# Sorted block attention and a feed-forward layer on one core: q of batch 1 loaded in rows and turned by TensorE, and w_in loaded in row blocks

## The chip, the cores and the metric

The kernel runs on one core of a Trainium2 chip. The metric is device time in microseconds; lower is better. The core has TensorE (PE; its weight loads are shown apart as PEld), VectorE (DVE), ScalarE (ACT), GpSimd (POOL) and SyncE (SP). POOL and SP also issue the DMA transfers here: POOL the loads, which turn f32 into bf16, SP the stores and the DMA transposes.

## The reference

Four batches of eight heads, 768 tokens, head size 64. A small matrix per head (8x8) is normalised five times over rows and columns and then mixes the eight blocks of 96 keys and of 96 values. Each block of 96 queries attends to its own mixed block. All heads of a token side by side are the input of a feed-forward layer with a leaky activation.

```python
P = sort_net                                   # (4, 8, 8, 8)
for _ in range(5):
    P = np.exp(P - np.max(P, axis=-1, keepdims=True))
    P = P / (np.sum(P, axis=-1, keepdims=True) + 1e-09)
    P = P / (np.sum(P, axis=-2, keepdims=True) + 1e-09)
k_sorted = np.einsum('bhij,bhjcd->bhicd', P, k_b)     # k_b, v_b: (4, 8, 8, 96, 64)
v_sorted = np.einsum('bhij,bhjcd->bhicd', P, v_b)
scores = np.matmul(q_b, k_sb.transpose(0, 1, 2, 4, 3)) / 8
...
x = attn_out.transpose(0, 2, 1, 3).reshape(3072, 512)
h = x @ w_in                                          # 512 x 2048
g = np.maximum(h, 0.0) + alpha * np.minimum(h, 0.0)
out = g @ w_out                                       # 2048 x 512
```

## The kernel before

**Order.** Nothing is issued in the order of the Python text. `G.add` records operations with an engine (or a choice of ACT and DVE, `EITHER`), an assumed duration, what they read and write, and a priority. A list scheduler (`schedule`) lays them out by priority and readiness, `search` tries 1,500 random shifts of the priorities and keeps the best layout by its own durations, and `emit` writes each engine's instructions in that order with semaphore waits. Each engine, and each of the two DMA-issuing engines, then works through its own list in order: an instruction that waits holds back everything behind it on its engine. `fill` puts matmuls whose result nobody uses into gaps of PE's list, ahead of the first FFN2 step.

**Loads.** POOL issues q, k and v of batch 0 first, in rows: the destination has 128 partitions with 3072 consecutive elements each (`QS`, `KS`, `VST`). Then come w_in in four blocks of 512 columns (L803; block `p` serves the FFN steps `ft` 4p to 4p+3), w_out in two, and k of batch 1. q of batches 1 to 3 goes another way (`load_q`): eight loads, one for each head, into `QN`, with tokens on partitions and 64 consecutive elements a piece, the other half of each 128 columns being zeros (L447).

**Turning q.** The scores need q with the head dimension on partitions (`QTz`). For batch 0, `prep_q` does it on PE: six steps of 16 matmuls of 64x64 against the identity (`pairs`, L540), each followed by a copy on ACT or DVE (L373). In this form one head lies on partitions 0 to 63 and another on 64 to 127, and a score matmul uses one half of the rows (L621). For batches 1 to 3, `turn_q` issues six DMA transposes on SP (L410). There the other 64 rows are zeros, and a score matmul uses all 128 rows (L618).

**k and v.** `prep_k` (six steps a batch, L540) and `prep_v` (eight steps, L583) mix the blocks by matmuls with `BDK`, a block matrix made of P. v is first rearranged by `conv_v` into `VD` (L373; from batch 1 on, all on POOL). From batch 1 on all these steps use one PSUM bank, `BANK_P`, the second bank of `psYP`: a step writes the bank, a copy on ACT or DVE empties it, and the next step follows.

**Attention.** 32 groups `g`, eight a batch, each a block of 96 queries in all heads. For batch 0 the scores are made twice (L621, then L642 and L633), exp is one ACT instruction (L665), and PE turns the result (L699). For batches 1 to 3 (`far`) exp is eight ACT instructions (L654), SP issues a DMA transpose of the weights (`ET`, L659), the output product follows (L674), and SP issues another DMA transpose into `xT` (L692).

**FFN.** Tokens go in chunks of 2, 2, and then 4 groups. `ffn1` (L721: four matmuls of 192 or 384 columns; then ACT L731 and DVE L734) makes one of 16 pieces `ft` of the hidden layer; `ffn2` (L760: four parts of four matmuls of 512 columns) makes 128 tokens of output, which are copied and stored (L774). These steps are put between the attention steps by their priorities.

Of the kernel before, what the change touches and what calls it, by code (L numbers as in the profile page):

```python
# [8 lines left out]
AP = bass.AP  # L9
# [9 lines left out]
DFF = 2048  # L19
KT_TILES = DM // 128  # L20
# [15 lines left out]
def t_pe(*mms):  # L36
    return sum(max(n, m, 64) / 2.4 + 4 for n, m in mms)
# [252 lines left out]
def bass_sinkhorn_attn__then__act_prelu_kernel(  # L290
# [11 lines left out]
    G = _Graph()  # L302
# [13 lines left out]
    EITHER = ("act", "dve")  # L316
# [55 lines left out]
    def copy(e, o, i):  # L372
        return e.activation(o, i, ACTF.Copy) if e is nc.scalar else e.tensor_copy(o, i)  # L373

    def t_either(n, mode=1):
        return {"act": t_act(n), "dve": t_dve(n, mode)}
# [17 lines left out]
        return [(("turned", "turnx")[n % 2], g + n // 2)]  # L394

    def load_q(b, prio):
        if b == 0:
            G.add(POOL, lambda e: e.dma_start(QS[0][:, :], AP(q.tensor, 0, [[3072, 128], [1, 3072]])),
                  load_us, w=[("QS", 0)], prio=prio, dma=(d_q[0], 0))
            return  # L400
        for h in range(H):
            G.add(POOL, lambda e, h=h: e.dma_start(  # L402
                AP(QN, h * 128 + (h // 4) * 64, [[6144, 128], [1024, 6], [1, 64]]),
                AP(q.tensor, b * HB + h * S * D, [[D, 128], [128 * D, 6], [1, D]])),
                660, r=[("QN0", h)] + paced(13, h // 2) * (b == 3), w=[("QN", h)], prio=prio,
                dma=(d_qn[h], 0))

    def turn_q(b, t, prio):
        n = b % 2
        G.add(SYNC, lambda e: e.dma_start_transpose(  # L410
            AP(QTz[n], t * 128, [[6144, 128], [768, 8], [1, 128]]),
            AP(QN, t * 1024, [[6144, 128], [1, 1024]])),
            4500, r=[("QN", h) for h in range(H)] + [("turned", 8 * b - 8 + t)] * (b > 1),
            w=[("QTzt", n, t)] + ([("Q0", u) for u in range(6)] if n == 0 and t == 0 else []),
            prio=prio, dma=(d_qt[t], 0))

    def load_kv(t, src, name, sem, g, b, prio):
# [125 lines left out]
            return inst  # L543
        return f

    def prep_q(u, prio, bank):
        t, off, row, keys = bank
        G.add(PE, pairs(QS[0], 0, u, identb, 0, 128, bank), 372, r=[("QS", 0), "identb"], w=keys, prio=prio)
        o = AP(QTz[0], 8 * u, [[6144, 128], [96, 32], [48, 2], [1, 8]])
        i = AP(t, off, [[row, 128], [2, 32], [1, 2], [64, 8]])  # L550
        G.add(EITHER, lambda e: copy(e, o, i), t_either(512), r=keys, w=[("Q0", u)], prio=prio)

    def prep_k(b, u, prio, bank=BANK_P):
        n = b % 2
# [14 lines left out]
    def conv_v(b, u, prio):  # L569
        o = AP(VD, 8 * u * 64, [[4096, 128], [64, 8], [1, 48]])  # L570
        i = AP(VST[b % 2], 8 * u, [[3072, 128], [1, 8], [64, 48]])
        G.add(POOL if b or u % 3 == 2 else EITHER, lambda e: copy(e, o, i), {"act": 858, "dve": 540, "pool": 720},
              r=[("VST", b % 2)] + [("VST", b % 2, x) for x in range(4)], w=[("VD", u)], prio=prio)

    def prep_v(b, u, prio, bank=BANK_P):
# [20 lines left out]
    def attention(g, prio):  # L596
# [2 lines left out]
        n, m = b % 2, g % 2  # L599
        far, me = b > 0, g % NE  # L600
        nk = 112
        pos = (lambda h4, hp: 2 * h4 + hp) if far else (lambda h4, hp: 4 * hp + h4)
        ld, bk = 4 * NB * BK0, BK0
        kt_keys = [("KT", n, u) for u in range(6)] + ([] if far else ["KTpad"])
        qt_keys = [("QTzt", n, t) for t in range(i * 96 // 128, (i * 96 + 95) // 128 + 1)] if far else \
            [("QTzt", n, t) for t in range(6)] + [("Q0", u) for u in range(6)]
        vs_keys = [("VS1", n)] + [("VS", n, u) for u in range(8)]
        psZ, psZb, banks_o = (psYP, psYPb, ["psY"] + PSP) if g == 1 else (psO, psOb, ["psO0", "psO1"])
        psX, banks_s = (psH, [("psH", x, y) for x in range(2) for y in range(2)]) if g == 1 else (psS, ["psS0", "psS1"])
# [1 line left out]
        def s1(e):  # L611
            inst = None
            for h4 in range(4):
                for hp in range(2):
                    p = pos(h4, hp)
                    o = AP(psX, (p // 4) * 512 + (p % 4) * 96, [[1024, 96], [1, 96]])
                    if far:
                        inst = e.matmul(o, AP(QTz[n], hp * 3072 + h4 * 768 + i * 96, [[6144, 128], [1, 96]]),  # L618
                                        AP(KT[n], (h4 * 8 + i) * bk, [[ld, 128], [64, 2], [1, 48]]))
                    else:  # L620
                        inst = e.matmul(o, AP(QTz[n], hp * 64 * 6144 + h4 * 768 + i * 96, [[6144, 64], [1, 96]]),  # L621
                                        AP(KT[n], hp * 64 * ld + (h4 * 8 + i) * bk, [[ld, 64], [64, 2], [1, 48]]))
            return inst
# [87 lines left out]
    def ffn1(ga, gb, ft, prio):  # L711
        tok, n = ga * BLK, (gb - ga) * BLK
        tb = step[0] % 3
        banks = BANK_H + ([BANK_P] if ga < 2 else [])
        pt, poff, _, keys = banks[step[0] % len(banks)]
        step[0] += 1

        def f(e):
            inst = None
            for kt in range(KT_TILES):  # L720
                inst = e.matmul(AP(pt, poff, [[1024, 128], [1, n]]),  # L721
                                AP(w_in_bf, kt * DFF + ft * 128, [[KT_TILES * DFF, 128], [1, 128]]),
                                AP(xT, kt * XR + tok % XR, [[KT_TILES * XR, 128], [1, n]]),
                                start=(kt == 0), stop=(kt == KT_TILES - 1))
            return inst
        op = G.add(PE, f, t_pe(*[(n, 128)] * 4), r=[("xT", g % 16) for g in range(ga, gb)] + [("w_in", ft // 4)],
              w=keys, prio=prio)
        if not ffn_ops:
            ffn_ops.append(op)

        G.add(ACT, lambda e: e.activation(AP(t1[tb], 0, [[384, 128], [1, n]]),  # L731
                                          AP(pt, poff, [[1024, 128], [1, n]]), ACTF.Relu, scale=-1.0),
              t_act(n), r=keys, w=[("t1", tb)], prio=prio)
        G.add(DVE, lambda e: e.scalar_tensor_tensor(  # L734
            out=AP(hT, ft * RING + tok % RING, [[FT_TILES * RING, 128], [1, n]]),
            in0=AP(t1[tb], 0, [[384, 128], [1, n]]), scalar=AP(omaT, ft, [[16, 128], [1, 1]]),
            in1=AP(pt, poff, [[1024, 128], [1, n]]), op0=AluOpType.mult, op1=AluOpType.add),
            t_dve(n) + 52, r=keys + [("t1", tb), "omaT"],
            w=[("hT", ft, x % (RING // 64)) for x in range(tok // 64, (tok + n) // 64)], prio=prio)
# [52 lines left out]
    sinkhorn()  # L792
    spread([0], -48)
    for u in range(6):
        prep_q(u, -50, (BANK_H + BANK_O + BANK_S)[u])
    for u in range(6):
        prep_k(0, u, -47, BANKS0[(u + 1) % 5])
    for u in range(8):
# [2 lines left out]
        prep_v(0, u, -45, (BANK_O + [BANK_P])[u % 3])  # L801
    for p in range(4):
        G.add(POOL, lambda e, p=p: e.dma_start(  # L803
            AP(w_in_bf, p * 512, [[KT_TILES * DFF, 128], [DFF, KT_TILES], [1, 512]]),
            AP(moe_w_in.tensor, p * 512, [[DFF, 128], [128 * DFF, KT_TILES], [1, 512]])),
            2550, w=[("w_in", p)], prio=-40 + p, dma=(dma_sem("wi%d" % p), 0))
    for p in range(2):
        G.add(POOL, lambda e, p=p: e.dma_start(
# [26 lines left out]
    for g in range(NG + 12):  # L835
        while fp < len(ffn_plan) and ffn_plan[fp][0] < g:
            pr, kind, a = ffn_plan[fp]
            if kind == 0:
                ffn1(*a, pr)
            else:  # L840
                ffn2(*a)
            fp += 1
        if g >= NG:
            continue
        b, i = g // NB, g % NB
        if i == 0 and b + 1 < B:
            if b == 0:
                load_k(1, -21)
            if b < 2:
                load_q(b + 1, 8 * b - 20)  # L850
            if b == 0:
                load_v(1, -19)
        attention(g, g)
        if g == 1:
            spread([1, 2, 3], 1)
        if b + 1 < B:
            for t in range(6 if b == 0 and i == 1 else 0):
                turn_q(1, t, 2 + t / 2)
            if b > 0 and i < 6:
                turn_q(b + 1, i, 8 * b + 2 + i / 2)  # L860
            vu = [(conv_v, b + 1, u) for u in range(3)]
            for u in range(8):
                vu += [(prep_v, b + 1, u)] + [(conv_v, b + 1, u + 3)] * (u < 5)
            units = [(prep_k, b + 1, u) for u in range(6)]
            units = units + vu if b == 0 else vu + units
            for x in range(len(units)):
                if i == (4 + x * 4 // len(units) if b == 0 else 1 + x * 7 // len(units)):
                    f, *a = units[x]
                    f(*a, 8 * b + 2 + x * 5 / len(units) if b else x / 4 if f is prep_k else 4.5 + x / 8)
        if i == 7 and b == 0:  # L870
            load_v(2, -12)
            load_k(2, -11.9)
        if g == 15:
            load_v(3, -4)
            load_k(3, -3.9)
            load_q(3, -2)
# [49 lines left out]
```

## Time and profile before

| | us |
|---|---|
| median of three runs | 256.91 |
| lowest and highest | 255.8, 257.92 |
| the profiled execution, device time | 259.23 |
| its span, from the first to the last instruction | 257.5 |

The profile is of one execution. Times in it count from the start of its span. Its mean granted clock of TensorE was 0.973. Of the span, PE was busy 93%, DVE 65%, ACT 60% and POOL 24%. The costliest groups of PE are the two FFN products (L721, 97.0 us; L760, 80.0 us on `psYP`). The DMA engines moved 32.17 MB in 77,070 packets, 67,808 of them under 512 bytes.

Some landings, from issue to the last byte: `QS` 7.1 us after issue at 1.3; the four w_in blocks 14.3, 16.3, 18.1 and 20.4 us after issues at 4.3, 5.1, 5.8 and 6.5; k of batch 1 31.8 us after 9.4; the eight `QN` loads of batch 1 27.8 us after the first issue (14.3) to some 24 us after the last (23.1); v of batch 1 26.7 us after 23.9. SP issued the six QTz transposes of batch 1 from 46.87 to 63.76 us.

How to read it: a line of the timeline has the start, the duration, the engine, the source line and the operation, with the tiles written and read and the count of merged instructions. A bracket gives idle time of the engine just before and what ended it. Matmuls overlap, so the distance between two starts says more about the cost of a step than its duration.

### The profile page before, as it was taken

To read this page: it belongs to the slowest core of one execution; us is meant where nothing else is said; L and a number is where in the kernel's file an instruction comes from. 1 tells how busy PE (TensorE), PEld (TensorE's weight loads), DVE (VectorE), ACT (ScalarE), POOL (GpSimd) and SP (SyncE) were. 2 spreads that over 40 slices of the span, in tenths; PEclk is the share of its full clock that TensorE was granted. 3 is DMA by queue.
4 is the path that set the end of the run, shared out by engine and by line. 5 is a ranking of instruction groups with operands and counts; after the bars stand their busy time and mean duration, and the time that the engine had idled before them with its cause. 6 is when DMAs were issued, how large, how long until landed. Compare 5 with 4: busy or idle time off the path is not lost.

```text
span 257.5 us, 6566 instructions
## 1 busy us (share of the span) xinstructions
PE 238.7 (93%) x2721; PEld 147.2 (57%) x2752; DVE 166.2 (65%) x330; ACT 154.1 (60%) x419; POOL 61.4 (24%) x89
## 2 busy tenths in 40 slices
PE   7687799979999997989899999999999999999995
PEld 4355577767656564645565565555555565555544
DVE  5773577666676896756887667466477795655510
ACT  4473444555775976758856654857667775555511
POOL 8999000194493020867100000000000000000000
PEclk9997779988999999999999999999999999999999
DMA  5999999999299989999985961212537234201112
GB/s 100 214 203 203 190 217 165 215 173 196 66 89 197 142 128 158 174 179 178 138 141 129 162 136 59 44 45 75 118 93 97 47 95 113 71 5 40 76 44 83
DMA packets 77070, 32.17 MB, mean 125 GB/s; under 512 B 67808, under 2 KB 73200, under 8 KB 77040
## 3 DMA queue, kind: packets, MB, share of 16 engines
q0 software_dynamic: 25168, 13.63, 40.8%
q1 hardware_dynamic: 51872, 18.11, 38.5%
q8 instruction: 21, 0.34, 0.6%
q14 instruction: 9, 0.07, 0.1%
HBM read 27.28 MB, written 6.29 MB: 130 GB/s over the span
## 4 chain that ended last, share of the span: by engine, by line
PE 76%; DMA 8%; POOL 6%; DVE 3%; issue 3%; ACT 3%; POOLq 0%
PE psH L721 28%; PE psYP L760 25%; DMA ET<-Esb 8%; PE psYP L583 4%; PE psS L760 3%; PE psO L674 3%; PE psS L618 3%; PE psS L633 2%; PE psYP L540 2%; ACT Esb L654 1%; POOL QN L447 1%; PE psYP L883 1%; POOL w_in_bf L803 1%; PE psS L642 1%; PE psO L583 1%
## 5 line engine op out<-in xcount | busy, mean ns | idle before, releaser
L734 DVE SCALAR_TENSOR_TENSOR hT<-t,omaT,psH 128x384 bf16<-128x384 f32 (+1 forms) x139 | 77.6, 572 | 41.2 <-ACT t L731 39.7
L721 PE MATMUL psH<-xT,w_in_bf 128*128 128x384 bf16 (+1 forms) x556 | 97.0, 312 | 0.9 <-DVE hT L734 0.7
L731 ACT ACTIVATE t<-psH 128x384 f32<-128x384 f32 (+1 forms) x139 | 62.3, 465 | 42.5 <-PE psH L721 39.8
L760 PE MATMUL psYP<-w_out_bf,hT 128*128 128x512 bf16 x306 | 80.0, 382 | 2.9 <-issue 1.3
L721 PEld LDWEIGHTS psH<-xT,w_in_bf 128*128 128x128 bf16 x556 | 50.9, 98 | 33.9 <-DVE hT L734 5.9
L654 ACT ACTIVATE Esb<-psS,nf 96x96 bf16<-96x96 f32 x192 | 46.3, 344 | 1.5 <-DVE nf L627 1.3
L760 PEld LDWEIGHTS psYP<-w_out_bf,hT 128*128 128x128 bf16 x336 | 30.6, 98 | 27.9 <-issue 0.6
L373 POOL COPY VD<-VST 128x384 bf16<-128x384 bf16 x26 | 22.6, 869 | 33.8 <-DMA VST<-in_v_dram 25.7
L627 DVE TENSOR_REDUCE nf<-psS 96x8 f32<-96x768 f32 x24 | 22.7, 948 | 2.1 <-PE psS L618 1.9
L684 DVE TENSOR_TENSOR xq<-psO,rec 96x512 bf16<-96x512 f32 x31 | 21.3, 687 | 1.1
L402 POOL DMA_DIRECT2D QN<-in_q_dram x24 | 19.8, 845 | 2.3 <-DMA xT<-xq 1.8
L373 ACT ACTIVATE outstg<-psYP 128x512 f32<-128x512 f32 x15 | 9.0, 597 | 12.7 <-PE psYP L760 12.7
L583 PE MATMUL psYP<-BDK,VD 128*64 128x64 bf16 x416 | 12.1, 202 | 3.5 <-issue 2.0
L681 DVE RECIPROCAL rec<-psO 96x8 f32<-96x8 f32 x31 | 6.2, 201 | 13.2 <-PE psO L674 13.1
L373 ACT ACTIVATE VS<-psYP 112x512 bf16<-112x512 f32 x14 | 9.7, 690 | 7.6 <-PE psYP L583 7.2
L583 PEld LDWEIGHTS psYP<-BDK,VD 128*64 128x64 bf16 x416 | 9.1, 114 | 8.6 <-issue 4.2
L618 PEld LDWEIGHTS psS<-KT,QTz 128*96 128x96 bf16 x192 | 11.6, 124 | 3.2 <-ACT Esb L654 0.4
L373 ACT ACTIVATE KT<-psYP 128x512 bf16<-128x512 f32 x13 | 7.8, 597 | 9.5 <-PE psYP L540 9.5
L618 PE MATMUL psS<-KT,QTz 128*96 128x96 bf16 x192 | 12.8, 209 | 0.0
L674 PEld LDWEIGHTS psO<-VS,ET 112*128 112x128 bf16 x192 | 8.6, 98 | 6.4 <-DMA ET<-Esb 3.0
L883 PE MATMUL psYP<-identb 128*128 128x512 bf16 x37 | 11.6, 438 | 0.3 <-ACT identb L373 0.3
L674 PE MATMUL psO<-VS,ET 112*128 112x65 bf16 x192 | 9.9, 194 | 1.6 <-DMA ET<-Esb 1.6
(116 smaller groups left out, 183.3 us busy)
## 6 DMA issues: line engine op xcount, KB each, us to landing
out_dram<-outstg SPq DMA_DIRECT2D x23, 256.0 KB, 2.3
KS<-in_k_dram POOLq DMA_DIRECT2D x3, 768.0 KB, 30.0
VST<-in_v_dram POOLq DMA_DIRECT2D x3, 768.0 KB, 26.7
QN<-in_q_dram POOLq DMA_DIRECT2D x24, 96.0 KB, 6.5
w_in_bf<-in_moe_w_in_dram POOLq DMA_DIRECT2D x4, 512.0 KB, 17.2
w_out_bf<-in_moe_w_out_dram POOLq DMA_DIRECT2D x2, 1024.0 KB, 27.1
QS<-in_q_dram POOLq DMA_DIRECT2D x1, 768.0 KB, 7.1
VST<-in_v_dram POOLq DMA_DIRECT2D x4, 192.0 KB, 5.4
```

Of the source, the lines that this page charges most:

```text
L373: return e.activation(o, i, ACTF.Copy) if e is nc.scalar else e.tensor_copy(o, i)
L402: G.add(POOL, lambda e, h=h: e.dma_start(AP(QN, h * 128 + (h // 4) * 64, [[6144, 128], [1024, 6], [1, 64]]), AP(q.tensor, b * HB + h * S * ...
L583: inst = e.matmul(AP(t, th * 64 * row + off + dd * 64, [[row, 64], [1, 64]]), AP(VD, (8 * u + dd) * 64, [[4096, 128], [1, 64]]), AP(BDK, b ...
L618: inst = e.matmul(o, AP(QTz[n], hp * 3072 + h4 * 768 + i * 96, [[6144, 128], [1, 96]]), AP(KT[n], (h4 * 8 + i) * bk, [[ld, 128], [64, 2], ...
L627: G.add(DVE, lambda e: e.tensor_reduce(AP(nx, 0, [[8, 96], [4, 2], [1, 4]]), AP(psX, 0, [[1024, 96], [512, 2], [96, 4], [1, 96]]), AxisLis ...
L654: inst = e.activation(AP(Esb[me], p * 128, [[1024, 96], [64, 2], [1, 48]]), AP(psX, (p // 4) * 512 + (p % 4) * 96, [[1024, 96], [48, 2], [ ...
L674: inst = e.matmul(AP(psZ, hp * 512 + h4 * 68, [[1024, 128], [1, 65]]), AP(ET[me] if far else Es0[m], pos(h4, hp) * 96, [[800, nk], [1, 128]]),
L684: G.add(DVE, lambda e: e.tensor_tensor(out=AP(xq[me], 0, [[512, 96], [256, 2], [64, 4], [1, 64]]), in0=AP(psZ, 0, [[1024, 96], [512, 2], [ ...
L721: inst = e.matmul(AP(pt, poff, [[1024, 128], [1, n]]), AP(w_in_bf, kt * DFF + ft * 128, [[KT_TILES * DFF, 128], [1, 128]]), AP(xT, kt * XR ...
L731: G.add(ACT, lambda e: e.activation(AP(t1[tb], 0, [[384, 128], [1, n]]), AP(pt, poff, [[1024, 128], [1, n]]), ACTF.Relu, scale=-1.0), t_ac ...
L734: G.add(DVE, lambda e: e.scalar_tensor_tensor(out=AP(hT, ft * RING + tok % RING, [[FT_TILES * RING, 128], [1, n]]), in0=AP(t1[tb], 0, [[38 ...
L760: inst = e.matmul(AP(bank[0], bank[1], [[1024, 128], [1, n]]), AP(hT, ft * RING + tok % RING, [[FT_TILES * RING, 128], [1, 128]]), AP(w_ou ...
```

## The change

q of batch 1 is now loaded as q of batch 0 is, by one load into `QS`, and turned by `prep_q` on PE into `QTz[1]`, with `BANK_P` as its bank. Its scores use the form with half of the rows; exp, the transposes of `ET` and `xT` and the output product stay as they were. Six DMA transposes and eight loads go. `turn_q` stays for batches 2 and 3, whose first step now waits for the readers of the earlier contents of that `QTz`. w_in is loaded in four blocks of 128 rows with all 2048 columns, and as a product needs all rows, each FFN1 step now depends on all four. The q steps of batch 1 are put between its k steps and its v steps, v with priorities from 4 on in place of 4.5, and the duration that the scheduler assumes for a VD copy on POOL goes from 720 to 870.

```diff
     def load_q(b, prio):
-        if b == 0:
-            G.add(POOL, lambda e: e.dma_start(QS[0][:, :], AP(q.tensor, 0, [[3072, 128], [1, 3072]])),
-                  load_us, w=[("QS", 0)], prio=prio, dma=(d_q[0], 0))
+        if b < 2:
+            G.add(POOL, lambda e: e.dma_start(QS[0][:, :], AP(q.tensor, b * HB, [[3072, 128], [1, 3072]])),
+                  load_us, w=[("QS", 0)], prio=prio, dma=(d_q[b], 0))
             return
...
-            w=[("QTzt", n, t)] + ([("Q0", u) for u in range(6)] if n == 0 and t == 0 else []),
+            w=[("QTzt", n, t)] + [("Q", n, u) for u in range(6)] * (t == 0),
...
-    def prep_q(u, prio, bank):
+    def prep_q(b, u, prio, bank=BANK_P):
         t, off, row, keys = bank
         G.add(PE, pairs(QS[0], 0, u, identb, 0, 128, bank), 372, r=[("QS", 0), "identb"], w=keys, prio=prio)
-        o = AP(QTz[0], 8 * u, [[6144, 128], [96, 32], [48, 2], [1, 8]])
+        o = AP(QTz[b], 8 * u, [[6144, 128], [96, 32], [48, 2], [1, 8]])
...
-        G.add(POOL if b or u % 3 == 2 else EITHER, lambda e: copy(e, o, i), {"act": 858, "dve": 540, "pool": 720},
+        G.add(POOL if b or u % 3 == 2 else EITHER, lambda e: copy(e, o, i), {"act": 858, "dve": 540, "pool": 870},
...
-        pos = (lambda h4, hp: 2 * h4 + hp) if far else (lambda h4, hp: 4 * hp + h4)
+        pos = (lambda h4, hp: 2 * h4 + hp) if b > 1 else (lambda h4, hp: 4 * hp + h4)
...
-                    if far:
+                    if b > 1:
                         inst = e.matmul(o, AP(QTz[n], hp * 3072 + h4 * 768 + i * 96, [[6144, 128], [1, 96]]),
                                         AP(KT[n], (h4 * 8 + i) * bk, [[ld, 128], [64, 2], [1, 48]]))
...
-        op = G.add(PE, f, t_pe(*[(n, 128)] * 4), r=[...] + [("w_in", ft // 4)],
+        op = G.add(PE, f, t_pe(*[(n, 128)] * 4), r=[...] + [("w_in", kt) for kt in range(KT_TILES)],
...
-            AP(w_in_bf, p * 512, [[KT_TILES * DFF, 128], [DFF, KT_TILES], [1, 512]]),
-            AP(moe_w_in.tensor, p * 512, [[DFF, 128], [128 * DFF, KT_TILES], [1, 512]])),
+            AP(w_in_bf, p * DFF, [[KT_TILES * DFF, 128], [1, DFF]]),
+            AP(moe_w_in.tensor, p * 128 * DFF, [[DFF, 128], [1, DFF]])),
...
-            for t in range(6 if b == 0 and i == 1 else 0):
-                turn_q(1, t, 2 + t / 2)
...
-            units = units + vu if b == 0 else vu + units
+            units = units + [(prep_q, 1, u) for u in range(6)] + vu if b == 0 else vu + units
...
-                    f(*a, 8 * b + 2 + x * 5 / len(units) if b else x / 4 if f is prep_k else 4.5 + x / 8)
+                    f(*a, 8 * b + 2 + x * 5 / len(units) if b else x / 4 if f is prep_k else 4 + x / 8)
```

The layout is searched anew, so the order of every engine's list changes around these steps too. In POOL's new list, v and q of batch 1 and then seven of the eight QN loads of batch 2 follow k of batch 1, ahead of v and k of batch 2 (before, the QN loads of batch 2 were issued at 71.4 to 78 us).

## The prediction

> **What bounds the kernel now.** The page first: busy shares, slices, and the head of the chain of waits.
>
> ```profile
> PE 238.7 (93%) x2721; PEld 147.2 (57%) x2752; DVE 166.2 (65%) x330; ACT 154.1 (60%) x419; POOL 61.4 (24%) x89
> ...
> PE   7687799979999997989899999999999999999995
> ...
> PEclk9997779988999999999999999999999999999999
> DMA  5999999999299989999985961212537234201112
> ...
> PE 76%; DMA 8%; POOL 6%; DVE 3%; issue 3%; ACT 3%; POOLq 0%
> ```
>
> PE is busy 93% of the span and holds 76% of the chain, while the DMA engines are full or nearly so (9 or 8) from 6 to 64 us and again from 71 to some 135 us. Transfers bind only through what PE waits for, and PE shows few such waits. Next the windows of PE after the first FFN step (32.21 us); columns: length, busy us of PE, PEld, DVE, ACT, POOL, granted clock, DMA share, GB/s.
>
> ```profile
> 52.00:57.00 5.00, 3.94 (x90) 3.10 (x92) 2.91 (x8) 2.44 (x5) 4.63 (x7) 0.96 1.09 192
> 57.00:60.00 3.00, 2.67 (x27) 1.79 (x28) 2.10 (x4) 1.25 (x4) 1.60 (x2) 0.50 1.67 176
> 60.00:72.00 12.00, 11.61 (x211) 8.74 (x211) 7.90 (x18) 9.03 (x26) 5.67 (x7) 1.00 0.47 101
> 72.00:90.00 18.00, 17.32 (x191) 10.32 (x191) 13.28 (x23) 12.94 (x40) 7.38 (x10) 1.00 1.44 153
> 90.00:104.00 14.00, 12.32 (x210) 7.79 (x213) 10.79 (x18) 10.03 (x32) 2.47 (x5) 1.00 1.10 148
> 104.00:130.00 26.00, 23.57 (x254) 13.81 (x253) 18.34 (x33) 18.25 (x57) 14.62 (x19) 1.00 1.47 162
> ```
>
> Idle PE time is 1.06 + 0.33 us in 52 to 60 and 1.68 + 2.43 us in 90 to 130; the other windows after 32 us have 0.3 to 1.1 each, up to the tail. So PE work that is added after 32 us lengthens the kernel by itself, and a gain must come out of those idle stretches. The prices, from PE's timeline: a step costs the distance from its start to the next start (the second number, its duration, also holds the drain).
>
> ```profile
> 46.97 0.44 PE L540 MATMUL psYP<-BDK,KS 64*64 64x64 bf16 x16
> 47.34 0.41 PE L674 MATMUL psO<-VS,Es 112*128 112x65 bf16 x8
> ...
> 48.71 0.38 PE L621 MATMUL psS<-KT,QTz 64*96 64x96 bf16 x8
> 49.02 0.34 PE L699 MATMUL psO<-identb,xq 96*128 96x96 bf16 x4
> ...
> 79.46 1.46 PE L721 MATMUL psH<-xT,w_in_bf 128*128 128x384 bf16 x8
> 80.76 0.52 PE L618 MATMUL psS<-KT,QTz 128*96 128x96 bf16 x8
> 81.21 0.44 PE L583 MATMUL psYP<-BDK,VD 128*64 128x64 bf16 x16
> 81.58 1.48 PE L721 MATMUL psH<-xT,w_in_bf 128*128 128x384 bf16 x8
> 82.99 0.44 PE L583 MATMUL psYP<-BDK,VD 128*64 128x64 bf16 x16
> ...
> 114.39 0.52 PE L618 MATMUL psS<-KT,QTz 128*96 128x96 bf16 x8
> 114.75 1.03 PE L760 MATMUL psYP<-w_out_bf,hT 128*128 128x512 bf16 x4
> ```
>
> Sixteen 64x64 matmuls (L540, the form of the q turns) cost 0.37 us. Scores in row halves (L621) cost 0.31, over the full array (L618) 0.36 here and up to 0.40. The same eight FFN matmuls take 1.30 us ahead of L618 and 1.41 ahead of L583: going over from a full-array step to one in a part of the array costs 0.10 us more. Ahead of L540, L621 and L642 the distances grow by 0.09 to 0.10 as well; the way back is free. The Trainium skill ("TensorEngine Tiling (Array Packing)", Key Properties) says that a change of tiling mode drains TensorE. The trace agrees, at 0.10 us; the page gives no price for it. Its table Theoretical Speedup has up to 2x for small contractions: eight scores in some 0.19 us, by which the sum below would be 1.0 us lower; L621's 0.31 does not agree.
>
> **The change, part by part.**
>
> *q turns on PE.* Six prep_q steps of batch 1: 6 x 0.37 = 2.22 us, in a stretch where PE has next to no idle time. Their six copies go to ACT, 0.57 us each (row of the QTz copies), 3.4 us in all; ACT is busy 1.25 + 9.03 of the 15 us from 57 to 72, 4.7 free, so I take nothing. If that cover were gone they would cost up to 3.4.
>
> *Scores of batch 1.* Eight groups from 0.36-0.40 to 0.31: 8 x 0.07 = -0.56 us.
>
> *Switches.* PE's order in the changed program goes from a full-array step to a partial one 55 times after the first FFN step, 46 times before: 9 x 0.10 = +0.90. With the scores that is +0.34: the row halves pay for themselves at most.
>
> *DMA transposes.* Six QTz transposes leave SP, where they held the queue from 46.87 to 63.76 us. The next in that queue is an output tile, which nobody waits for. The first score of batch 1 (68.08 us) shows no wait for QTz. I take 0; at most the two waits on ET below.
>
> *q loads.* Eight QN loads (landing one after another from 42.1 us, the last at 46.9, 5.7 us behind k of batch 1 at 41.2) become one QS load with rows like KS and VST, which land 3.8 us apart (v of batch 1 at 50.6, then 54.4 and 58.2). In POOL's new order v of batch 1 goes ahead of it: k lands at 41.2 as before, v at 45.0, q at 48.8. The first prep_q stands after the K steps, near 54, so q comes in time by some 5 us. The QN loads of batch 2 move from 71.4-78 us to POOL's early list; q's six turns no longer hold QN. v and k of batch 2 then land near 58 and 61, v as before (58.2) for VD copies that now come later.
>
> *Waits on ET.* PE idled 0.75 us at 113.3 and 0.49 at 126.3 for ET transposes, beside loads and QTz transposes. With the QN packets out of 71-83 and the turns of batch 2 no longer waiting for them the attention groups run earlier; loads of batch 3 stay. Between 0 and -1.24 I take half, -0.62.
>
> *A gap filled.* The first q turn stands between L699 and L642 of group 6, a place that was 0.45 us long for 0.18 us of work: -0.27.
>
> *w_in in row blocks.* Every first FFN step now needs all four blocks. They landed at 18.6, 21.4, 23.9 and 26.9, 2.75 us apart; first use 32.21. A block of 512 KB would take 2.5 us by the KS rows (3.8 for 768 KB) and 3.8 by the QN loads (5.7 for 768 KB); counted from 15.85, one old block ahead of the first landing, the last lands between 25.9 and 31.1, in time by either: 0.
>
> *The end.* The last group's output product (L674, 220.24) is followed in the old order by 7.6 us of PE work that doesn't need its xT, in the new one by 0.25 + 1.30 + 3 x 0.86 = 4.15. xT came 4.5 us after that product (transpose issued at 222.44, landed 2.3 later): +0.35.
>
> Sum: 2.22 - 0.56 + 0.90 + 0.35 - 0.62 - 0.27 = +2.02 us. The profiled execution took 259.23 (span 257.5), so 261.25 on its own terms; it lies 2.32 above the median, near the size of one 2.03 us stall of PE for nothing shown (19.2 us, followed by a clock of 0.62) that I assume for neither side. On the median: 256.91 + 2.02 = 258.9.
>
> **The rivals.**
>
> *Faster: the gaps close.* Half-speed clock followed the idle stretch: 57 to 60 ran at 0.50, which cost some 1.3 us. The Trainium skill ("TensorE: Matmul & The Clock Gate", Part 1) says that the gate follows recent activity over windows of 3.4 us; the rows agree. If the q turns keep PE busy there and lighter queues end the waits in 90 to 130, all of 1.39 + 1.3 + 4.11 = 6.8 us goes: 256.91 + 2.22 - 0.56 + 0.90 + 0.35 - 6.8 = 253.0. For it: POOL, SP and the early queue are relieved. Against: most of that idle time ends on ACT or DVE emptying a bank (KT 0.69, outstg 0.42, VS 0.30 each, hT 0.41 and 0.31), and the change adds such copies. Chance 0.15.
>
> *Slower: one PSUM bank.* K, q and V of batch 1 all go through BANK_P, a matmul step and then a copy: 20 steps now instead of 14. Before, 14 starts spread from 46.97 to 72.56, 1.97 us each; where they stood closest, 1.14 to 1.39. In the new order the last V step stands on PE near 81 us, so the chain decides from (81 - 47) / 19 = 1.79 us a step on. At 1.97 it ends at 84.4: 3.4 us more, 262.3. Against: FFN steps between them set much of the 1.97. Chance 0.20.
>
> *w_in late.* It decides when a block takes over (32.21 - 15.85) / 4 = 4.1 us; each 0.1 us beyond costs 0.4, and at 4.5 the time is 260.5. The slowest row above is 3.8. Chance 0.03.
>
> **How the numbers follow.** 1% is 2.57 us, about what a measurement of this kernel tells from no change: 254.3 to 259.5. The forecast has 0.62, with its own range 256.8 to 261 (waits on ET in full or none, ACT's copies partly bare). A third or so of it lies above 259.5; with the bank and w_in this makes slower 0.38, the gaps make faster 0.15, and 0.47 is within. 254.0 to 262.5 leaves out the best of the first rival and the worst of the second.
>
> **What would show it.** In the page after: PE busy up by 2 to 3 us, L540 with 96 matmuls more that read QS, L618 at 128 and L621 at 120, QTz transposes 12. No wait of L540 for QS, none of L721 for w_in. FFN steps ahead of the scores of batch 1 at 0.10 us more. ET waits near 113 and 126 gone or halved, and L721 waiting some tenths for xT behind the last L674. I am wrong if PE's idle time between 52 and 130 (5.5 us in those four windows) falls by more than 3 us, or if prep_v steps of batch 1 wait on VS or QTz copies for more than 2 us together.

## The result, and the profile after

| | before | after |
|---|---|---|
| median, us | 256.91 | 259.34 |
| lowest and highest of the runs behind it | 255.8, 257.92 | 258.86, 261.15 |
| the profiled execution, device time | 259.23 | 259.97 |
| its span, mean granted clock | 257.5, 0.973 | 258.3, 0.974 |

The ratio is 1.0102, 95% interval 1.0058 to 1.0146: 2.6 us more, between 1.5 and 3.8. Every ratio and interval in this document leaves out the executions that lie over 1.5% above the fastest of their kernel (one of the five of before, ten of the twelve of before_seed8 further down), while the medians in the table of experiments are of all executions. Set side by side, the two profiled executions differ by only 0.7 us, because that of before lay 2.3 above its median and that of after 0.6.

The page of after, busy shares, slices and the head of the chain of waits:

```profile
PE 241.0 (93%) x2816; PEld 147.5 (57%) x2850; DVE 165.8 (64%) x332; ACT 156.3 (61%) x423; POOL 54.7 (21%) x82
...
PE   7688799979999998999999999999999999999995
...
PEclk9996779989999999999999999999999999999999
DMA  5999999994029788999988781231343233310112
...
PE 77%; DMA 9%; ACT 6%; DVE 4%; issue 2%; SPq 0%; POOL 0%
```

PE is busy 2.3 us longer with 95 matmuls more. The DMA row shows the place of the packets that are gone: the tenth to twelfth slice (58 to 77 us) fall from 9, 2 and 9 to 4, 0 and 2. PE's share of the chain did not get smaller by it (76% before). The same windows as before (length, busy us of PE, PEld, DVE, ACT, POOL, granted clock, DMA share, which adds up the times of packets and can pass 1, and GB/s):

```profile
52.00:57.00 5.00, 4.02 (x88) 3.10 (x84) 2.58 (x6) 3.04 (x6) 0.05 (x1) 0.89 1.06 216
57.00:60.00 3.00, 2.67 (x37) 1.68 (x40) 1.97 (x4) 1.41 (x4) 0.00 (x0) 0.61 1.05 144
60.00:72.00 12.00, 11.63 (x221) 8.84 (x220) 6.83 (x17) 9.43 (x27) 2.56 (x3) 1.00 0.08 26
72.00:90.00 18.00, 16.96 (x239) 9.79 (x234) 12.88 (x22) 12.69 (x35) 5.27 (x7) 1.00 0.68 108
90.00:104.00 14.00, 12.76 (x186) 7.29 (x189) 10.63 (x18) 9.86 (x33) 1.65 (x4) 1.00 0.85 121
104.00:130.00 26.00, 24.55 (x275) 14.42 (x278) 19.13 (x33) 19.46 (x61) 14.82 (x19) 1.00 1.45 171
```

Idle PE time in 52 to 60 and 90 to 130 is 0.98 + 0.33 + 1.24 + 1.45 = 4.0 us, 1.5 less than before. The turns and the new switches, from PE's timeline of after (start, duration, then the step):

```profile
52.90 0.34 PE L699 MATMUL psO<-identb,xq 96*128 96x96 bf16 x4
53.66 0.44 PE L540 MATMUL psYP<-identb,QS 64*64 64x64 bf16 x16 [0.41 <-ACT KT L373]
54.03 0.41 PE L642 MATMUL psS<-QTz,KT 64*112 64x96 bf16 x8
...
59.84 0.44 PE L540 MATMUL psYP<-identb,QS 64*64 64x64 bf16 x16
60.21 0.41 PE L642 MATMUL psS<-QTz,KT 64*112 64x96 bf16 x8
...
108.74 1.46 PE L721 MATMUL psH<-xT,w_in_bf 128*128 128x384 bf16 x8
110.13 0.38 PE L621 MATMUL psS<-KT,QTz 64*96 64x96 bf16 x8
110.44 0.44 PE L540 MATMUL psYP<-BDK,KS 64*64 64x64 bf16 x16
```

A turn costs 0.37 us (59.84 to 60.21), a score group of batch 1 now 0.31 (110.13 to 110.44), and an FFN1 step of eight matmuls ahead of it 1.39 in place of 1.30. The first turn waited 0.41 us for the bank. Of PE's waits in after, summed over the kernel (us in total, times, the longest):

```profile
PE psH L721 <- DVE hT L734: 1.1, 3, 0.5
...
PE psYP L540 <- DVE KT L373: 0.5, 1, 0.5
PE psYP L540 <- ACT KT L373: 0.4, 1, 0.4
PE psO L674 <- DMA ET<-Esb: 0.4, 1, 0.4
...
PE psYP L583 <- DVE VS L373: 0.2, 1, 0.2
```

The three ET waits of before (1.6 us) are one of 0.4. No turn of batch 1 waits for QS and no FFN1 step for w_in. Of the bank's waits 0.41 and 0.16 us fall into the preparation of batch 1; the 0.5 belongs to batch 2.

Counting from the first FFN1 step (32.21 us before, 31.75 after) to the end of the last PE step (254.85, 255.61), after takes 223.86 us and before 222.64. Taking all start-to-start distances of that stretch, less the idle time printed in brackets, PE's steps come to 216.06 before and 218.38 after, its idle time to 6.58 and 5.48. So the work grew by 2.3 us, and gaps took up 1.1 of it in these two executions. Of the idle time 1.3 and 1.4 us stand ahead of L760 with no releaser, and they are in doubt: these two traces have 369 and 366 of the 400 matmuls of L760, and the four traces that have all 400 show no such idle time.

### The profile page after: what moved, and what is told of

Same layout as the page of the kernel before. It is cut to its first block, busy times and chain, and to the rows that moved or that the text cites. A ratio compares the mean times of both kernels' runs of the same rounds, so it can differ in the third digit from the quotient of the medians.

```text
span 258.3 us, 6752 instructions
## 1 busy us (share of the span) xinstructions
PE 241.0 (93%) x2816; PEld 147.5 (57%) x2850; DVE 165.8 (64%) x332; ACT 156.3 (61%) x423; POOL 54.7 (21%) x82
## 4 chain that ended last, share of the span: by engine, by line
PE 77%; DMA 9%; ACT 6%; DVE 4%; issue 2%; SPq 0%; POOL 0%
PE psH L721 29%; PE psYP L760 25%; DMA VST<-in_v_dram 5%; PE psS L760 3%; PE psYP L540 3%; PE psO L674 3%; ACT Esb L654 3%; PE psYP L583 3%; PE psS L633 2%; PE psS L618 2%; DMA ET<-Esb 2%; ACT t L731 2%; PE psYP L881 1%; DVE hT L734 1%; PE psS L621 1%
## 5 line engine op out<-in xcount | busy, mean ns | idle before, releaser
L760 PE MATMUL psYP<-w_out_bf,hT 128*128 128x512 bf16 x303 | 78.7, 382 | 3.4 <-issue 1.4
L721 PEld LDWEIGHTS psH<-xT,w_in_bf 128*128 128x128 bf16 x556 | 50.2, 98 | 34.9 <-DVE hT L734 5.9
L760 PEld LDWEIGHTS psYP<-w_out_bf,hT 128*128 128x128 bf16 x336 | 30.4, 98 | 29.3 <-issue 0.5
L373 POOL COPY VD<-VST 128x384 bf16<-128x384 bf16 x26 | 22.9, 879 | 42.4 <-PE psYP L583 22.5
L373 ACT ACTIVATE outstg<-psYP 128x512 f32<-128x512 f32 x16 | 9.6, 597 | 14.3 <-PE psYP L760 14.3
L402 POOL DMA_DIRECT2D QN<-in_q_dram x16 | 13.3, 853 | 7.0 <-DMA xT<-xq 5.7
L373 DVE CAST VS<-psYP 112x512 bf16<-112x512 f32 x11 | 7.6, 689 | 7.6 <-PE psYP L583 7.6
L373 ACT ACTIVATE VS<-psYP 112x512 bf16<-112x512 f32 x15 | 10.3, 688 | 3.3 <-PE psYP L583 2.9
L583 PE MATMUL psYP<-BDK,VD 128*64 128x64 bf16 x416 | 11.7, 200 | 0.2 <-DVE VS L373 0.2
L583 PEld LDWEIGHTS psYP<-BDK,VD 128*64 128x64 bf16 x416 | 8.8, 113 | 5.3 <-issue 2.9
L373 ACT ACTIVATE KT<-psYP 128x512 bf16<-128x512 f32 x12 | 7.2, 596 | 6.2 <-PE psYP L540 6.1
L618 PEld LDWEIGHTS psS<-KT,QTz 128*96 128x96 bf16 x128 | 7.9, 124 | 2.8 <-ACT Esb L654 0.8
```

The source lines that it names most:

```text
L402: G.add(POOL, lambda e, h=h: e.dma_start(AP(QN, h * 128 + (h // 4) * 64, [[6144, 128], [1024, 6], [1, 64]]), AP(q.tensor, b * HB + h * S * ...
L583: inst = e.matmul(AP(t, th * 64 * row + off + dd * 64, [[row, 64], [1, 64]]), AP(VD, (8 * u + dd) * 64, [[4096, 128], [1, 64]]), AP(BDK, b ...
L721: inst = e.matmul(AP(pt, poff, [[1024, 128], [1, n]]), AP(w_in_bf, kt * DFF + ft * 128, [[KT_TILES * DFF, 128], [1, 128]]), AP(xT, kt * XR ...
L760: inst = e.matmul(AP(bank[0], bank[1], [[1024, 128], [1, n]]), AP(hT, ft * RING + tok % RING, [[FT_TILES * RING, 128], [1, 128]]), AP(w_ou ...
```

## The experiments

Each run stands beside runs of the kernel before on the same chip; their medians were 257.78, 259.03 and 257.84 in the three sittings. Ratios are to those.

| kernel | median, us | ratio and 95% interval |
|---|---|---|
| after_again (w_in in columns) | 259.18 | 1.0088, 1.0045 to 1.0130 |
| q_twice | 262.72 | 1.0187, 1.0123 to 1.0252 |
| q_one | 259.12 | 1.0044, 1.0003 to 1.0085 |
| full_rows | 259.43 | 1.0079, 1.0037 to 1.0121 |
| w_rows_alone | 257.93 | 1.0019, 0.9976 to 1.0062 |
| copy_doubled | 260.27 | 1.0133, 1.0080 to 1.0187 |
| before_seed8, after_seed8 | 259.05, 255.70 | 0.9943 (0.9848 to 1.0038), 0.9922 (0.9875 to 0.9969) |
| before_seed9, after_seed9 | 256.97, 259.27 | 0.9947 (0.9899 to 0.9995), 1.0074 (1.0036 to 1.0112) |
| before_seed10, after_seed10 | 255.95, 260.46 | 0.9935 (0.9891 to 0.9978), 1.0116 (1.0067 to 1.0166) |

### w_in's shape, both ways

after_again is the changed kernel with the old transfers of w_in, w_rows_alone the old kernel with the new ones. All engines' lists stay as they were.

```diff
# after_again, against after
-            AP(w_in_bf, p * DFF, [[KT_TILES * DFF, 128], [1, DFF]]),
-            AP(moe_w_in.tensor, p * 128 * DFF, [[DFF, 128], [1, DFF]])),
+            AP(w_in_bf, p * 512, [[KT_TILES * DFF, 128], [DFF, KT_TILES], [1, 512]]),
+            AP(moe_w_in.tensor, p * 512, [[DFF, 128], [128 * DFF, KT_TILES], [1, 512]])),
# w_rows_alone, against before: the reverse, and
-        ... + [("w_in", ft // 4)],
+        ... + [("w_in", kt) for kt in range(KT_TILES)],
```

> The changed kernel with one thing undone: w_in is transferred in four blocks of 512 columns again; every FFN1 step still depends on all four, and every engine's list is the changed kernel's. Theory (PE work sets the time, w_in's shape costs nothing): the same time as the changed kernel, 259.3 within 0.5 us, first FFN1 step at 31.7 us within 0.3. Rival (the row blocks cost or gain something, by landing times or by what larger packets do to other queues): more than 1 us off 259.3, with the first FFN1 step or PE's early stall moved by as much.

> The kernel before with w_in alone loaded in four row blocks, every FFN1 group waiting for all four; the lists of all engines are those of before. Theory (the rise comes from the work and the order on PE after 32 us; w_in's shape is worth nothing): within 0.5 us of before, ratio 0.998 to 1.002; POOL's four issues of w_in take 2.1 instead of 3.0 us, no L721 waits for w_in. Rival (the row blocks cost DMA time or a wait): 1 us or more slower, with the first FFN1 later than 32.2.

Ratios 1.0088 against the change's own 1.0102, and 1.0019 against 1: both are within their intervals of no effect, and that of w_rows_alone ends at 1.0062, 1.6 us. In the trace POOL's four issues of w_in take 2.13 us instead of 3.00, no FFN1 step waits for w_in, and the first one starts at 32.08 (32.21 before). The row blocks save 0.9 us on POOL, which shows in no wait of PE. In after_again the first FFN1 step starts at 32.31, 0.6 us later than in after and outside the 0.3 that I expected. It shows no wait for w_in either; the granted clock was 0.50 there for 17 us from 20.5, and in after for 7 from 22.

So the rise comes from the rest of the change: q's new way and the order that goes with it. The moved v steps and the longer assumed VD copy were not tried apart.

These two kernels are also second executions of the same lists. From the first FFN1 step to the last PE step, w_rows_alone took 221.41 us (32.08 to 253.49) and after_again 223.91 (32.31 to 256.22): 2.5 apart, as the medians are, where the first two profiles had 1.2. The steps come to 215.52 and 219.32 us, the idle time to 5.88 and 4.58.

### The turns: doubled, and replaced

```diff
# q_twice
+        def turns(e):
+            for _ in range(2 if b == 1 else 1):
+                inst = turn(e)
+            return inst
# q_one: q of batch 1 is not turned; one product of 512 columns a step stands in
+            return e.matmul(AP(t, off, [[row, 128], [1, 512]]), identb[:, :],
+                            AP(QS[0], 8 * u * 64, [[3072, 128], [1, 512]]))
```

> The changed kernel with the sixteen matmuls of each q turn of batch 1 issued twice; lists and result unchanged. Theory (PE work after 32 us lengthens the kernel by itself): 6 x 0.37 = 2.2 us more than the changed kernel, 261.5 within 0.6. Rival (the q turns lie in gaps of PE, and the change's loss is from the order of the lists): under 0.7 us more.

> The changed kernel with the sixteen matmuls of each q turn of batch 1 replaced by one full-array matmul of 512 columns, so that q of batch 1 is not turned and its scores are of other numbers; lists unchanged. Theory: a turn goes from 0.37 to 0.22 us and four of the six entries into a partial form (0.10 each) go: 6 x 0.15 + 0.4 = 1.3 us less than the changed kernel, 258.0 within 0.6. Rival (the turns are hidden): within 0.4 us of 259.3.

q_twice lies 0.0099 above after_again in the same sitting, 2.5 us, and 0.0085, 2.2 us, above the ratio of after; by the medians it is 3.5 us, and 262.72 lies above the 261.5 within 0.6 that I expected. The six turns are on the path, nothing hides them all. Two places of its timeline:

```profile
61.94 0.69 PE L540 MATMUL psYP<-identb,QS 64*64 64x64 bf16 x32
62.56 0.83 PE L727 MATMUL psH<-xT,w_in_bf 128*128 128x192 bf16 x8
...
107.43 0.40 PE L680 MATMUL psO<-VS,ET 112*128 112x65 bf16 x8 [1.55 <-DMA ET<-Esb]
```

The doubled step costs 0.62, so the sixteen additional matmuls cost 0.25 by themselves, 1.5 us in six; the other 0.12 of a single turn's 0.37 doesn't double. The measured 2.2 to 2.5 is more than 1.5, by no more than the intervals leave open. Part of it need not be the turns themselves: in this execution PE waited 2.8 us for ET, 1.55 of it in the last line, and 0.65 in after_again. q_one lies 0.0044 below after_again by the ratio (1.1 us, 1.3 expected), but the medians differ by 0.06 only, and the intervals overlap: its direction is not settled. Its product step costs 0.34 by the trace, close to a turn. With the switches ahead of them all six steps save 0.6 us there, so it was a weaker contrast than I had meant.

### The row halves

full_rows makes the scores of batch 1 over all 128 rows, which adds up two heads where the kernel keeps them apart; the turns and all lists stay.

```diff
+                    elif b == 1:
+                        inst = e.matmul(o, AP(QTz[n], h4 * 768 + i * 96, [[6144, 128], [1, 96]]),
+                                        AP(KT[n], (h4 * 8 + i) * bk, [[ld, 128], [64, 2], [1, 48]]))
```

> The changed kernel with the scores of batch 1 over all 128 rows instead of a half, so that each is the sum of two heads' scores; lists unchanged. Theory (row halves pay for themselves at most: 0.31 + 0.10 for the entry against 0.36 to 0.40): within 0.5 us of the changed kernel's 259.3, and L618-like distances of 0.36 to 0.40. Rival (row halves are worth their 0.07 each without the entry, or two run side by side): 0.6 to 1.5 us more than 259.3.

1.0079 against 1.0088: 0.2 us less, the intervals almost the same. By the distances the eight groups take 3.81 us here and 2.69 in after_again. Three of them cost the 0.36 to 0.40 that I expected, the others 0.45 to 0.70, where a partial step or a wait comes next. What the row halves gain at the scores goes back to the switches: in the kernel these stand ahead of a score group, in full_rows behind it (54 entries into partial steps, 55 in the kernel).

### The copies behind the turns

```diff
+        def copies(e):
+            if b == 1:
+                copy(e, o2, i)      # o2: columns of QTz[1] that batch 1 does not use
+            return copy(e, o, i)
-        G.add(EITHER, lambda e: copy(e, o, i), t_either(512), r=keys, w=[("Q", b, u)], prio=prio)
+        G.add(EITHER, copies, t_either(512), r=keys, w=[("Q", b, u)], prio=prio)
```

> The changed kernel, with the copy of each turned q unit of batch 1 out of PSUM done twice by its engine (the first time into columns of QTz[1] that batch 1 does not use). Six more copies of about 0.6 us on the vector or scalar engine between 54 and 66 us. Theory (the copies lie under work of PE): 0 to 0.5 us over the changed kernel, ratio to before about 1.008 to 1.012. Rival (one PSUM bank turn after turn: product, copy, product; the copy is on the path): up to six times 0.6 = 3.6 us more, ratio about 1.022.

0.8 us over the ratio of after and 1.2 over after_again, where the theory had 0 to 0.5 and the rival 3.6. The timeline of ACT, and the two steps of PE that waited for such a copy:

```profile
57.72 1.08 ACT L373 ACTIVATE QTz<-psYP 128x512 bf16<-128x512 f32 x2 [0.17 <-PE psYP L540]
...
59.59 1.13 ACT L373 ACTIVATE QTz<-psYP 128x512 bf16<-128x512 f32 x2
```

```profile
55.87 0.50 PE L726 MATMUL psYP<-xT,w_in_bf 128*128 128x192 bf16 x4 [0.31 <-ACT QTz L373]
...
60.78 0.44 PE L540 MATMUL psYP<-identb,QS 64*64 64x64 bf16 x16 [0.38 <-ACT QTz L373]
```

Five doubled copies ran on ACT and one on DVE, and PE waited for two of them, 0.31 and 0.38 us. The first wait took the place of another in part: the wait for Es behind it was 0.19 us, in after it was 0.57. A chain through the single bank is excluded (1.022 lies above the interval's end of 1.0187); that the copies are wholly free is not shown.

### The order that the search finds

The planner's random search was started from three other numbers, for both kernels. The operations are the same; the order differs in places on every engine.

```diff
-        rng = random.Random(7)
+        rng = random.Random(8)      # 9, 10
```

> The kernel before, its planner's random search started from another number (8 for 7): the same operations, in an order that differs in places. Theory (amount of PE work sets the time): within 1.5 us of before. Rival (the time hangs on which order the search happens to find): 2 us or more from before, on either side.

> The changed kernel with the search started from 8. Theory (the change adds about 2 us of work to PE under any order): 2.0 us, give or take 1, above before_seed8 and within 1.5 us of the changed kernel. Rival (the measured 2.6 us are the order that the search found, by chance): the difference to before_seed8 leaves 0 to 4 us, and may change its sign.

> The kernel before, its planner's search started from 9. In PE's list 49 entries from a full-array step into a partial one after the first FFN step (46 in before, 50 in before_seed8). Theory after the seed-8 pair: the order that the search finds moves the time by about 2 us either way, and the change's own price shows in the mean of the pairs only. So 255 to 259 us. Rival (the search hardly matters and the seed-8 pair was noise): within 1 us of before.

> The changed kernel, search started from 9; 54 entries into partial steps. By the added PE work alone (2.2 for the turns, -0.6 for the scores, five entries at 0.1) 2.1 us above before_seed9. By the rival, that the gaps of the layout take up the turns, 0 or less.

> The kernel before, search started from 10; 49 entries. Theory as for before_seed9: 255 to 259 us.

> The changed kernel, search started from 10; 53 entries. By the added PE work alone 2.0 us above before_seed10 (2.2 - 0.6 + 0.4); by the rival 0 or less. Over the four pairs (7, 8, 9, 10) the theory has a mean difference of 1 to 2 us with a scatter of 2, the rival a mean near 0.

| pair | change by the ratios, us | change by the medians of the same executions, us | entries into partial steps | PE idle after the first FFN1, us |
|---|---|---|---|---|
| 7 | +2.6 | +2.6 | 46, 55 | 6.58, 5.48 |
| 8 | -0.5 | -1.2 | 50, 55 | 8.78, 5.46 |
| 9 | +3.3 | +3.6 | 49, 54 | 6.61, 6.44 |
| 10 | +4.7 | +4.5 | 49, 53 | 8.38, 6.63 |

(The ratio of a pair is that of its two ratios, times 257.) The mean is +2.5 by the ratios and +2.4 by the medians, where I had expected 1 to 2. The ratio of before_seed8 has the widest interval of all, 1.9%, so its pair is the least sure one; by the medians of the table of experiments it falls by 3.4, and the mean of the four is +1.5. Both theories were partly right. Three pairs rise by 2 to 5 us and one falls. Their scatter (a standard deviation of 2.2 us) leaves the mean of four uncertain by about 1.1, so a price of about 2 us fits them and is not pinned down by them. And the order alone moves one kernel by as much: by the ratios the three other orders of before are 1.4 to 1.7 us faster than the one in use (two of the three intervals lie below 1), and after_seed8, at 0.9922, beats both kernels of this study. My expectation for seed 8, 2.0 us within 1, fell, and so did that after_seed8 would lie within 1.5 us of the changed kernel.

Idle time fell with the change in every pair, by 0.2 to 3.3 us. The gaps do close, as the first rival said, most of all in pair 8. One place of before_seed8 shows how much a gap can hold; its PE timeline, and the windows around it:

```profile
121.27 0.82 PE L721 MATMUL psH<-xT,w_in_bf 128*128 128x384 bf16 x4
123.97 0.82 PE L721 MATMUL psH<-xT,w_in_bf 128*128 128x384 bf16 x4 [1.88 <-DMA xT<-xq]
...
126.53 2.65 PE L721 MATMUL psH<-xT,w_in_bf 128*128 128x384 bf16 x8
```

```profile
122.00:126.00 4.00, 1.82 (x31) 1.12 (x32) 0.79 (x2) 2.73 (x11) 0.00 (x0) 0.94 2.31 121
126.00:130.00 4.00, 3.95 (x28) 2.13 (x30) 2.69 (x5) 1.96 (x5) 0.00 (x0) 0.63 0.05 9
```

PE waited 1.88 us for xT with the DMA engines full, and the granted clock then fell: an FFN1 step took 2.65 us where it takes 1.46. Whether the wait brought the lower clock is open. A longer one in before_seed10 did not: the granted clock stayed at 1.00 behind it.

```profile
115.79 0.42 PE L674 MATMUL psO<-VS,ET 112*128 112x65 bf16 x8 [2.99 <-DMA ET<-Esb]
```

That the place of before_seed8 makes the difference within pair 8 was not tried apart.

## Why the prediction was right

The forecast was +2.0 us and the measurement +2.4 by the medians, +2.6 (1.5 to 3.8) by the ratio. The main step, that PE work added after the first FFN1 step lengthens the kernel by itself, held: doubling the turns alone cost 2.2 to 2.5 us, 1.5 of it in PE's steps. Term by term, with the profiles of before and after first and those of w_rows_alone and after_again as the second pair:

| term | forecast, us | what the runs show |
|---|---|---|
| six q turns | +2.22 | 0.37 a turn at full clock; 2.53 in all by the distances, with one turn at half clock |
| score groups of batch 1 | -0.56 | the distances of all L618 and L621 groups: 10.25 + 1.81 before, 6.93 + 4.48 after, so -0.65; in the second pair -1.2 |
| nine more switches | +0.90 | 1.39 for 1.30 ahead of L621. All steps but turns and scores: up by 0.4, in the second pair by 2.7, so their sum does not settle this term. full_rows: with the scores, about nothing |
| waits on ET | -0.62 | 1.6 to 0.4, so -1.2, the far end of the bounds; in the second pair 0.6 and 0.65, so nothing, the near end |
| the filled gap | -0.27 | did not come about |
| the end | +0.35 | did not come about |
| copies, QTz transposes, q loads, w_in | 0 | w_in 0 both ways; no wait for QS; copies nearly hidden; the transposes were not tried apart |

Two terms failed and cancelled each other in part. *The gap filled*: the distance from L699 to L642 of group 6 was 0.45 us before, and with the turn in it should have grown by 0.10. It grew to 1.13 (52.90 to 54.03), by 0.68, because the turn uses BANK_P and had to wait 0.41 us for the copy of the K step before it. I had counted only PE's time in the gap and not the bank; the second rival, with this very bank, had named it. It is not one wait more, though: in before the last K step waited 0.39 us just ahead of the same place.

```profile
53.48 0.44 PE L540 MATMUL psYP<-BDK,KS 64*64 64x64 bf16 x16 [0.39 <-ACT KT L373]
53.85 0.34 PE L699 MATMUL psO<-identb,xq 96*128 96x96 bf16 x4
54.30 0.41 PE L642 MATMUL psS<-QTz,KT 64*112 64x96 bf16 x8
```

*The end*: I forecast a wait for xT in the shorter stretch behind the last output product. The timelines of after, PE first, then DVE and SP's queue:

```profile
226.19 0.41 PE L674 MATMUL psO<-VS,ET 112*128 112x65 bf16 x8
226.43 1.47 PE L721 MATMUL psH<-xT,w_in_bf 128*128 128x384 bf16 x8
227.74 2.75 PE L760 MATMUL psYP<-w_out_bf,hT 128*128 128x512 bf16 x12
230.33 1.46 PE L721 MATMUL psH<-xT,w_in_bf 128*128 128x384 bf16 x8
```

```profile
225.40 1.26 DVE L734 SCALAR_TENSOR_TENSOR hT<-t,omaT,psH 128x384 bf16<-128x384 f32 x2 [0.90 <-ACT t L731]
226.64 0.20 DVE L681 RECIPROCAL rec<-psO 96x8 f32<-96x8 f32 x1
...
227.59 1.18 SPq L692 DMA_TRANSPOSE xT<-xq  x1
```

The same of before, where the product started at 220.24:

```profile
220.32 1.26 DVE L734 SCALAR_TENSOR_TENSOR hT<-t,omaT,psH 128x384 bf16<-128x384 f32 x2 [0.90 <-ACT t L731]
221.50 0.20 DVE L681 RECIPROCAL rec<-psO 96x8 f32<-96x8 f32 x1
...
222.44 1.18 SPq L692 DMA_TRANSPOSE xT<-xq  x1
```

4.14 us were left, as forecast (0.25 + 1.30 + 3 x 0.86 make 4.13, not 4.15), and no wait stands in the last line of PE. The 4.5 us that xT took were those of the old order, where the reciprocal stood behind a 1.26 us hT step on DVE and the transpose was issued 2.20 us after the product. In the new one the hT step had begun before the product and was over at 226.64; the issue came after 1.40 us, and with 2.3 us to landing xT was there after 3.7. I had carried a whole latency from one order to another when a part of it was a queue.

The forecast took an even effect of half-speed clock, and the second pair bears this out: the half-speed stretch at 57 us, which the first rival wanted to win back, is there in before and after and missing in w_rows_alone and after_again (below), so it belongs to the execution and not to the change.

*The rivals.* The gaps closed by 1.1 of the 6.8 us that the first rival needed, and in 52 to 60 and 90 to 130 us by 1.5, where 3 would have shown me wrong. The bank's twenty steps ran from 45.53 to 79.98 us, 1.81 us apart, right at the 1.79 from which I let it decide; but they were spaced by the FFN steps between them, and the waits for a copy came to 0.6 us, against 0.7 before. The distance between the steps was a poor threshold; the waits were the better witness. w_in was never late. In the chances, a third of 0.62 with the 0.20 and the 0.03 makes 0.44 for slower, not 0.38.

A forecast of one layout hit within 0.5 us what four layouts scatter over by several. The mean of the pairs, 2.5 us give or take 1.1, agrees with the price. That this layout shows it so exactly is in part luck: the wait on ET, the largest of the waits in the sum, went from one end of its bounds to the other between two pairs of executions of the same lists.

## What to carry to other kernels

In this kernel, with one engine busy 93% of the span, work moved onto it cost about its start-to-start distance, whatever queues it relieved. Look for what ends the idle stretches, and count the buffer as well as the engine before filling one. A latency read from one order is a sum of waits and work, so take it apart before carrying it over. And where a search lays out the program, compare several layouts of both kernels: here another start of the search was worth as much as the change.

## What the runs showed that I had not expected

**The granted clock differs between executions of the same list.** The 87 runs of before had mean clocks from 0.960 to 0.987, and their times follow:

| mean clock | 0.987 | 0.980 | 0.973 | 0.967 | 0.960 |
|---|---|---|---|---|---|
| runs | 14 | 10 | 24 | 28 | 11 |
| median, us | 255.9 | 257.0 | 257.7 | 259.2 | 260.5 |

4.7 us from end to end, nearly twice the change. At equal mean clock the change is still there: the executions of after and after_again have medians of 258.5 us at 0.987 (4), 259.2 at 0.980 (8) and 260.5 at 0.973 (4), 2.2 to 2.8 above those of before. The windows of before, then of w_rows_alone (the same lists), then of after_again (the lists of after):

```profile
26.00:32.20 6.20, 4.73 (x90) 3.40 (x84) 3.67 (x8) 2.69 (x5) 0.00 (x0) 0.74 1.20 194
```

```profile
26.00:32.20 6.20, 5.19 (x77) 3.61 (x72) 3.45 (x8) 2.35 (x4) 0.00 (x0) 0.50 1.21 198
...
57.00:60.00 3.00, 2.84 (x64) 2.17 (x64) 2.89 (x8) 2.52 (x6) 1.52 (x3) 1.00 1.48 174
```

```profile
26.00:32.20 6.20, 5.19 (x71) 3.39 (x70) 2.60 (x6) 1.91 (x4) 0.00 (x0) 0.50 1.22 197
...
57.00:60.00 3.00, 2.65 (x52) 1.86 (x54) 2.42 (x6) 2.29 (x7) 0.00 (x0) 1.00 1.00 147
```

Read in half-microsecond windows, half-speed stretches lasted some 7 us from 22 us, 3.5 from 32.5 and 3.5 from 56.5 in before; 14 in one piece from 22.5 in w_rows_alone; 17 in one piece from 20.5 in after_again; and a single one of some 3.4 from 29 in before_seed10. All are near multiples of 3.4 us, and the steps between the mean clocks above, 0.0065 of 257 us, are half of 3.4. The Trainium skill ("TensorE: Matmul & The Clock Gate", Part 1) has a window of about 3.4 us that runs freely and does not reset with the kernel, so that what it catches varies from run to run; the traces agree, and add what it does to a time.

**A stall with no releaser, and what lands ahead of its end.** PE stood still for 1.82 us ahead of 20.57 us in after and 2.03 ahead of 21.23 in before, with no releaser, in the midst of a V step of equal matmuls (L583):

```profile
20.57 0.28 PE L583 MATMUL psO<-BDK,VD 128*64 128x64 bf16 x6 [1.82 <-issue]
```

```profile
21.23 0.25 PE L583 MATMUL psYP<-BDK,VD 128*64 128x64 bf16 x4 [2.03 <-issue]
```

It is not chance: it stands ahead of the same matmul in every profiled execution of a list (after and the five kernels with its lists: six matmuls before the end of a step; before and w_rows_alone: four), with lengths from 1.27 to 2.27 us. A half-speed stretch began within 0.3 to 1.7 us of its end in all of these. In before_seed10 it was 0.31 us long with a second of 0.77 at 26 us, and the only half-speed stretch began at 29.

The traces say more of what PE waits for. In all 14 profiled executions the stall stands behind 705 or 706 recorded instructions of PE and PEld, whatever the list, and in the three other orders of before, which have a second one, that stands 256 or 257 further on. The profile's pages list a DMA queue, q8, as "instruction", with packets of 16 KB, and each of these stalls ended 1.3 to 1.5 us after such a packet had landed: at 19.19 us in after, 19.76 in before, 18.66 and 24.60 in before_seed10. So PE most likely waited there for its next block of instructions. It is argued from the places and times alone; no run moved such a block.
